# A two-layer transformer kernel whose order comes from a planner: own PSUM bank for the transposes of x, three early loads of x, a split last F pair, quartered output, and a new table of priorities

## The chip, the cores and the metric

The kernel runs on one core of a Trainium2 chip. The metric is device time in microseconds for one execution, lower is better; the profile's span, from the first to the last instruction, is a little shorter. PE is the matrix engine (PEld its weight loads), DVE the vector engine, ACT the scalar engine, POOL GpSimd, and SP the engine that here issues all DMAs.

## What is computed

Two kinds of layer alternate, four in all, on x of 2048 rows and 512 columns, float32:

```python
x = x + attention(layernorm(x), wqkv) @ wo          # 32 heads of 16; each row sees 8 rows: itself, -2, -4, ... -14
x = x + (gelu(xn @ w_gate) * (xn @ w_up)) @ w_down  # xn = layernorm(x), F = 1792
# the same two again, with the same weights
```

The text calls one attention and one feed-forward together a layer: layer 0 and layer 1.

## The kernel before

**Chunks.** Attention steps by 2, so even and odd rows never mix. `CHUNKS` (L38) cuts each layer into 8 chunks of 256 rows of one parity, each of J = 2 tiles of 128 rows. A chunk goes through three stages, for each of which a function adds nodes to a graph: `attention_inputs` (L1015), `attention` (L1092), `feed_forward` (L1229).

**Precision by halves.** Every product is made of float16 parts: an operand is split into hi and lo, and hi*hi + hi*lo + lo*hi is summed (`passes`, L1008), three matmuls for one. Weights are scaled by a power of two from their largest value, then split into hi and lo: `absmax` and `abssum` (L561, L570) find the largest value or a bound, `exponents` (L460) turns it across the partitions with PE, `split` (L513) makes hi on ACT (L520) and lo on DVE (L525). Activations are split and transposed in `split_transpose` (L955): ACT copies hi (L962), POOL subtracts lo (L966), then a DMA transposes both (L971), or, for the first tiles (`pt` = 6 of them), PE does (L981) and ACT copies the result from PSUM to `ax` (L988).

**attention_inputs.** x is loaded (`load_xa`, L824; into the buffers `x` instead of `xa` for the chunks in `early`, L1429), normed (statistics on DVE, L880; a chain of small steps on POOL, L937 to L952; ACT applies it, L1000), split, transposed, and multiplied by w_qkv in halves h of the heads: per tile and h two banks of `pg`, 512 and 256 columns (L1050). ACT copies them to `sc` (L1076), and SP stores them to DRAM as `qkvd` (L1085).

**attention.** For each of 4 groups of 8 heads SP loads q, k and v with the windows' rows (L1115), DVE multiplies and sums (L1138, L1147), softmax follows on DVE and ACT, DVE multiplies by v and sums (L1205, L1217). All products go through `prod`, one buffer of 128 x 2048 float32. The result is split and transposed into `ot`, one buffer.

**feed_forward.** PE multiplies `ot` by w_o (L1011, 512 columns), DVE adds to x (L1254), a second norm and transpose give `bx`. Then 7 pairs u of F blocks: gate and up on PE (L1011, 24 matmuls of 256 columns each), gelu on ACT (L1305), the product on DVE (L1312), sums of blocks on POOL (L1322 to L1324), which make 7 blocks out of 4 for a scheme with 7 products in place of 8, hi on ACT (L1332) and lo on POOL (L1337) into one of three buffers `gh`, and 21 matmuls with w_down into the banks `pd` (L1346). After the last pair DVE gathers six times from `pd` into x (L1375), and SP stores it (L1388): to `xs` after layer 0, to the output after layer 1, for the last chunk in two pieces.

w_down's raw rows are likewise turned into 7 blocks (`prep_d`, L694): for five pairs in place, and for the last two in halves s of 128 columns, with a temporary buffer each (L756: s = 0 in the second `bx`, s = 1 in `sc`).

**PSUM.** Eight banks: three `pg` of its own, one `pe` for the softmax, four `pd`. Until 196 us of the plan (`retire`), the four `pd` serve as other things: pd0, pd1 and pd3 as three more buffers of `pg`, pd2 as `pt`, which takes the transposes of x (L981), those of `exponents` (L473) and the warming matmuls (`unread`, L1407, L1411). Names in the profile are those of the bank, so a projection into one of them reads `pd`.

**What sets the order.** `Graph.plan` (L206) is a list scheduler that runs when the kernel is built: of all nodes whose inputs are there it takes the one that can start first by its cost model, and among those that can start together the one of lowest priority number. Costs are `t_act`, `t_dve`, `t_dvp`, `t_pool`, `t_mm` (L296 to L317), and `LAG` (L104) is the time from an instruction's end until another engine may use its result. The table `AT` (L52) holds the priorities: for instance `x0` for x of chunk 0, `lq0` and `lq1` for the loads of w_qkv, `pq`, `pf`, `po`, `pd` for the preparation of the weights, `start` and `step` for the chunks' own time T. Each engine then runs its list in order; semaphores come from the data.

## Time and profile before

| | |
|---|---|
| median of 3 runs | 1246.38 us (1244.66 to 1246.49) |
| profiled execution, its own time | 1246.04 us |
| its span | 1244.3 us |
| granted clock of PE, mean | 0.987 |
| idle time of PE in the span | 43.5 us |
| moved by DMA | 174.76 MB, 140 GB/s over the span |

A row of instructions gives line, engine, operation, output <- input, shape and count, then busy time, mean of one in ns, idle time of the engine before them and what ended it. A row of waits gives who waited for whom: time in total, times, longest. A row of a timeline gives start, length and instructions merged. SPq is SP's issuing of DMAs, "DMA bx<-hl" a transfer.

### The profile page before, as it was taken

The numbers are of one execution on the slowest core, as the hardware profiler recorded it, in microseconds if no ns is written. First come the engines' busy times: TensorE is split into PE (matmuls) and PEld (weight loads), VectorE is DVE, ScalarE is ACT, GpSimd is POOL, SyncE is SP. The second block draws the span as 40 slices with busy tenths as digits, with TensorE's granted clock in tenths as the row PEclk, the third lists the DMA queues.
The fourth block names the chain that finished last, engine by engine and source line by source line (L and its number), as shares of the span: only waits on it lengthen the run. The fifth ranks groups of instructions, "written<-read, shape, count | busy, mean of one in ns | idle before, by whom it ended". The sixth has DMA issues, their size and how long they took to land.

```text
span 1244.3 us, 24043 instructions
## 1 busy us (share of the span) xinstructions
PE 1200.8 (97%) x9722; PEld 954.1 (77%) x9722; DVE 935.5 (75%) x972; ACT 542.0 (44%) x911; POOL 690.2 (55%) x839
## 2 busy tenths in 40 slices
PE   3899989999999999999999999999999999999997
PEld 1455658887888778885688878878788888788886
DVE  7999998799868988517877867789788688775121
ACT  5787654434443435323443433434352625343211
POOL 3233426665666458553485936765476657465543
PEclk7899999999999999999999999999999999999999
DMA  9878783345533494208923346343834344241000
GB/s 337 280 246 202 205 224 117 128 146 144 159 115 127 137 252 107 94 2 232 235 96 100 128 138 165 101 145 115 241 104 118 100 132 124 100 124 43 18 18 18
DMA packets 195791, 174.76 MB, mean 140 GB/s; under 512 B 101904, under 2 KB 162656, under 8 KB 195680
## 3 DMA queue, kind: packets, MB, share of 16 engines
q1 hardware_dynamic: 195680, 173.23, 47.8%
q8 instruction: 76, 1.25, 0.4%
q14 instruction: 35, 0.29, 0.1%
HBM read 115.87 MB, written 33.73 MB: 120 GB/s over the span
## 4 chain that ended last, share of the span: by engine, by line
PE 84%; DMA 5%; DVE 4%; POOL 3%; issue 2%; ACT 1%; SPq 0%; POOLq 0%; DVEq 0%; ACTq 0%
PE pg L1011 51%; PE pd L1346 20%; PE pg L1050 9%; PE pd L1050 3%; DMA ax<-hl 2%; POOL hl L966 1%; DMA bx<-hl 1%; DMA xa<-xs 1%; DMA ot<-hl 1%; PE pd L1011 1%; DMA kv<-qkvd 1%; DVE prod L1138 1%; DMA w_d<-in_A_wqkv_dram 1%; POOL nw L938 0%; DVE w_q L525 0%
## 5 line engine op out<-in xcount | busy, mean ns | idle before, releaser
L1011 PE MATMUL pg<-bx,w_g 128*128 128x256 f16 x2664 | 310.6, 273 | 5.1 <-DMA bx<-hl 5.1
L1011 PE MATMUL pg<-bx,w_u 128*128 128x256 f16 x2664 | 309.0, 273 | 0.0
L1011 PEld LDWEIGHTS <-w_g 128*128 128x128 f16 x2688 | 263.6, 98 | 39.2 <-issue 5.6
L1011 PEld LDWEIGHTS <-w_u 128*128 128x128 f16 x2688 | 263.0, 98 | 30.6
L1050 PEld LDWEIGHTS <-ax 128*128 128x128 f16 x1536 | 151.5, 99 | 111.0 <-issue 12.0
L1050 PE MATMUL pg<-w_q,ax 128*128 128x512 f16 (+1 forms) x1152 | 203.0, 334 | 6.3 <-DVE w_q L525 4.2
L1312 DVE SCALAR_TENSOR_TENSOR sc<-pg,small,sc 128x512 f32<-128x512 f32 (+1 forms) x127 | 85.1, 680 | 157.7 <-PE pg L1011 143.1
L1305 ACT ACTIVATE sc<-pg,small 128x512 f32<-128x512 f32 (+1 forms) x127 | 78.8, 633 | 224.3 <-PE pg L1011 186.7
L1217 DVE TENSOR_REDUCE o<-prod 128x256 f32<-128x2048 f32 x64 | 146.1, 2282 | 36.2 <-POOL hl L966 33.7
L1322 POOL TENSOR_TENSOR sc<-sc 128x256 f32<-128x256 f32 x112 | 100.4, 896 | 127.0 <-DVE sc L1312 120.9
L1138 DVE TENSOR_TENSOR prod<-kv,q 128x2048 f32<-128x2048 f32 x64 | 152.6, 2385 | 7.8 <-DMA kv<-qkvd 7.1
L1205 DVE TENSOR_TENSOR prod<-kv,pe 128x1024 f32<-128x1024 f32 x128 | 152.6, 1216 | 1.4
L1147 DVE TENSOR_REDUCE lg<-prod 128x128 f32<-128x2048 f32 x64 | 145.7, 2277 | 0.6
L966 POOL TENSOR_TENSOR hl<-o,hl 128x256 f16<-128x256 f32 x64 | 59.2, 926 | 109.9 <-ACT hl L962 109.5
L1337 POOL TENSOR_TENSOR w_u<-sc,w_u 128x896 f16<-128x896 f32 x37 | 78.0, 2108 | 32.9 <-ACT w_u L1332 32.8
L1375 DVE SCALAR_TENSOR_TENSOR x<-pd,small,x 128x512 f32<-128x512 f32 x96 | 70.5, 743 | 32.9 <-PE pd L1346 31.4
L1337 POOL TENSOR_TENSOR w_g<-sc,w_g 128x896 f16<-128x896 f32 x37 | 76.2, 2059 | 32.7 <-ACT w_g L1332 32.4
L1346 PE MATMUL pd<-w_d,gh 128*128 128x256 f16 x798 | 93.5, 273 | 0.0
L1337 POOL TENSOR_TENSOR gh<-sc,gh 128x896 f16<-128x896 f32 x38 | 76.1, 2003 | 29.8 <-ACT gh L1332 29.6
L1346 PE MATMUL pd<-w_d,w_u 128*128 128x256 f16 x777 | 91.0, 273 | 0.0
L1346 PE MATMUL pd<-w_d,w_g 128*128 128x256 f16 x777 | 90.9, 273 | 0.0
L1324 POOL TENSOR_TENSOR sc<-sc 128x256 f32<-128x256 f32 x112 | 83.6, 747 | 8.8
(126 smaller groups left out, 1395.2 us busy)
## 6 DMA issues: line engine op xcount, KB each, us to landing
kv<-qkvd SPq DMA_DIRECT2D x128, 576.0 KB, 3.9
qkvd<-sc SPq DMA_DIRECT2D x64, 384.0 KB, 3.9
q<-qkvd SPq DMA_DIRECT2D x64, 128.0 KB, 3.5
x<-in_A_x_dram SPq DMA_DIRECT2D x9, 512.0 KB, 5.5
xs<-x SPq DMA_DIRECT2D x8, 512.0 KB, 4.8
xa<-xs SPq DMA_DIRECT2D x16, 256.0 KB, 3.8
x<-xs SPq DMA_DIRECT2D x8, 512.0 KB, 4.6
xa<-in_A_x_dram SPq DMA_DIRECT2D x14, 256.0 KB, 4.5
```

Source lines behind the costliest of these rows:

```text
L1011: nc.tensor.matmul(pt, a, b, start=i == 0, stop=i == n - 1)
L1050: nc.tensor.matmul(pgs[n].tile()[:, 0 : hi - lo], a[:, i // 2, kt], part(h * KT + kt)[:, lo:hi], start=(i, kt) == (0, 0), stop=(i, kt) == ...
L1138: nc.vector.tensor_mul(prod, win, q.tile().unsqueeze(2).to_broadcast([P, J, W, P]))
L1147: lambda lgv=lgv, heads=heads: nc.vector.tensor_reduce(lgv()[:, :, heads].rearrange("p j h w -> p j w h"), prod.rearrange("p j w (h d) -> ...
L1205: nc.vector.tensor_mul(paired[:, j].rearrange("p q (h d) t -> p q t h d", d=DH), win, by.unsqueeze(4).to_broadcast([P, W // 2, 2, HPG, DH]),)
L1217: lambda o=o: nc.vector.tensor_reduce(o.tile(), paired.rearrange("p j q c t -> p j c q t"), axis=AX.XY, op=ALU.add),
L1305: lambda sel=sel, h=h, part=part, g_of=g_of: nc.scalar.activation(g_of()[:, sel], part(0, sel), AF.Gelu_apprx_tanh, scale=cst["s_gate", h],),
L1312: lambda sel=sel, h=h, part=part, g_of=g_of: nc.vector.scalar_tensor_tensor(g_of()[:, sel], part(1, sel), cst["c_up", h], g_of()[:, sel], ...
L1322: tt(b[:, 4:6], b[:, 0:2], b[:, 3:4].to_broadcast([P, 2, P]), op=ALU.add)
L1324: tt(b[:, 1:3], b[:, 1:3], b[:, 0:4:3], op=ALU.subtract)
L1337: lambda blocks=blocks, gh_of=gh_of: nc.gpsimd.tensor_sub(gh_of()[:, 1], blocks(), gh_of()[:, 0]),
L1346: nc.tensor.matmul(pds_[PD_AT[m][0]].tile()[:, PD_AT[m][1]], gh_of()[:, a, G_AT[m]], wd_of(u, m, b), start=u == 0 and n == 0 and PD_AT[m][ ...
```

## The change

The pieces, in the order of the diff:

- `AT` has new values throughout and new entries: an offset for each chunk's inputs, attention and feed-forward (`I`, `A`, `F` with layer and chunk), for its groups of heads (`B`), for each pair of w_down (`D`), and a second value (`_2`) of 16 knobs, which holds from chunk 4 of layer 0 on (`turn` = 4; `knob` reads it).
- The planner's costs: DVE's and ACT's instructions are shorter by about 0.08 and 0.1 us, and their results come later by as much.
- `pg` has five buffers in the first stretch instead of six; pd3 becomes `px`, which takes the transposes of x alone. `retire` is at 161.55 us.
- The second halves of the last two pairs of w_down take `prod` as their temporary buffer.
- The first nodes of PE-transposed splits, the transposes, the gate and up matmuls, and the gelus are each kept in program order; w_o's product is planned after x has been asked for.
- `early` = 2: x of chunks 1 and 2 is loaded into the buffers `x`, that of chunk 0 as before into `xa`.
- In the last pair of the last chunk, blocks 0 and 3, which the sums leave as they are, get hi and lo ahead of the sums; the products 4 and 3, which need these alone, no longer wait for the other blocks.
- The output of the last chunk is stored in four quarters (a tile's 256 columns each) as each is gathered, the last of them by ACT.

Some priorities as they come out of the table, before and after: x of chunk 0 -1647 and -2454 (its two tiles), after -6653 and -6508; first load of w_qkv -6025, after -5513; w_o -1505, after -3790; gate matmuls of chunk 0 from 137, after from 2653; first projections of chunk 5 (-18.49 + 138.98 x 10 + 981.86 - 329.66 + 164.47) at 2188, their second half 740 later; those of chunk 6 (856.27 + 183.11 x 12 - 1471.81 + 1267.42 + 164.47) at 3014.

The core of the diff:

```diff
-    lq0=-6024.71, lq1=-3848.17, lf0=-1122.81, lo=-1504.86, lf1=-880.86, ld=-724.89, pq0=-2261.26, pq1=1109.7,
-    pf0=-58.05, po=-50.3, pf1=863.38, pd=596.57, x0=-1647.47, first=117.89, tile=80.47, ahead=10.4, lead=1240.39,
...
+    lq0=-5512.9, lq1=-2937.45, lf0=-1635.77, lo=-3790.27, lf1=-2793.33, ld=5813.67, pq0=-2542.65, pq1=-5324.02,
+    pf0=-2904.78, po=2529.52, pf1=-399.99, pd=3361.46, x0=-8823.93, first=-18.49, tile=138.98, ahead=10.4,
+    lead=3679.49, norm=10434.96, proj=164.47, half=740.13, row=247.98, att=-1559.49, hg1=-5.5, hg2=-93.36,
...
-LAG = {"PE": 0.25, "DVE": 0.07, "ACT": 0.1, "POOL": 0.12, "SP": 0.0}
+LAG = {"PE": 0.25, "DVE": 0.15, "ACT": 0.2, "POOL": 0.16, "SP": 0.0}
...
-    return 0.19 + 0.093 * ptr + n / 1200
+    return 0.09 + 0.093 * ptr + n / 1200
...
-    return (n + 151) / 960
+    return (n + 72) / 960
...
     P_pg = Pool(
-        "pg", [ps.tile([P, 512], F32, name=f"pg{i}") for i in range(3)] + banks(pds[0], pds[1], pds[3]),
+        "pg", [ps.tile([P, 512], F32, name=f"pg{i}") for i in range(3)] + banks(pds[0], pds[1]),
         fifo=False,
     )
     P_pt = Pool("pt", banks(pds[2]), fifo=False)
+    P_px = Pool("px", banks(pds[3]), fifo=False)
...
-            at = prio + AT["pdu"] * u
+            at = prio + AT["pdu"] * u + AT.get(f"D{u}", 0)
...
             for s in range(2):
-                sc = Lease(P_sc) if s else Lease(P_bx, only=(1,))
+                sc = Lease(P_pr) if s else Lease(P_bx, only=(1,))
                 blocks = lambda sc=sc, s=s: (
-                    sc.tile() if s else sc.tile().rearrange("p j t k c -> p (j t k c)").bitcast(F32)[:, 0 : 7 * P]
-                ).rearrange("p (m c) -> p m c", m=7)
+                    sc.tile().rearrange("p j w c -> p (j w c)") if s
+                    else sc.tile().rearrange("p j t k c -> p (j t k c)").bitcast(F32)
+                )[:, 0 : 7 * P].rearrange("p (m c) -> p m c", m=7)
                 cols_of = slice(s * P, (s + 1) * P)
...
+    def knob(name, l, c):
+        return AT.get(name + "_2", AT[name]) if 8 * l + c >= AT.get("turn", 4) else AT[name]
...
+    heads, turned_last, in_turn = [], [], {}
...
-        g.add(
+        first = g.add(
             "ACT", t_act(n), lambda: nc.scalar.copy(hi(), src()),
-            r=src_keys, w=[(lease, 0)], get=[lease], prio=prio,
-        )
+            r=src_keys, w=[(lease, 0)], get=[lease], prio=prio, order=heads[-1:] if on == "PE" else (),
+        )
+        if on == "PE":
+            heads.append(first)
         g.add(
...
-        pt = Lease(P_pt)
+        pt = Lease(P_px)
...
             "PE", 2 * nb * 0.06, turn, r=[(lease, 0), (lease, 1)], w=[(pt, 0)], get=[pt], prio=prio, urgent=True,
+            order=turned_last[-1:],
         ))
+        turned_last.append(turns[-1])
...
-                g.add(
+                in_turn["pg"] = g.add(
                     "PE", 24 * t_mm(N), columns,
                     r=[*((bx, j) for j in range(J)), *((key, h * KT + k) for h in hs for k in range(KT))],
-                    w=[(pgs[n], 0)], get=[pgs[n]], prio=T + AT["gu"] * J * u + 0.01 * n,
+                    w=[(pgs[n], 0)], get=[pgs[n]], prio=T + knob("gu", l, c) * J * u + 0.01 * n,
+                    order=[in_turn.get("pg")],
...
+            direct = last and u == NU - 1
+            if direct:
+                ends = lambda t: t[:, 0:4:3]
+                g.add(
+                    "ACT", t_act(2 * P),
+                    lambda blocks=blocks, gh_of=gh_of: nc.scalar.copy(ends(gh_of()[:, 0]), ends(blocks())),
+                    r=gk, w=[(gh, 0, 0)], get=[gh], prio=ev,
+                )
+                g.add(
+                    "POOL", t_pool(2 * P),
+                    lambda blocks=blocks, gh_of=gh_of: nc.gpsimd.tensor_sub(
+                        ends(gh_of()[:, 1]), ends(blocks()), ends(gh_of()[:, 0])
+                    ),
+                    r=[*gk, (gh, 0, 0)], w=[(gh, 1, 0)], prio=ev,
+                )
             if u >= AT["sd"]:
                 g.add("POOL", 2 * t_pool(2 * P) + t_pool(P) + 0.21, sums, w=gk, prio=ev)
             else:
                 g.add("DVE port", 2 * t_dve(2 * P) + t_dve(P), sums, w=gk, prio=ev)
-            g.add(
-                "ACT", t_act(7 * P),
-                lambda blocks=blocks, gh_of=gh_of: nc.scalar.copy(gh_of()[:, 0], blocks()),
-                r=gk, w=[(gh, 0)], get=[] if hold else [gh], prio=ev,
-            )
-            g.add(
-                "POOL", t_pool(7 * P),
-                lambda blocks=blocks, gh_of=gh_of: nc.gpsimd.tensor_sub(
-                    gh_of()[:, 1], blocks(), gh_of()[:, 0]
-                ),
-                r=[*gk, (gh, 0)], w=[(gh, 1)], prio=ev,
-            )
+            for k, cut in enumerate((slice(1, 3), slice(4, 7)) if direct else (slice(0, 7),)):
+                n = (cut.stop - cut.start) * P
+                g.add(
+                    "ACT", t_act(n),
+                    lambda blocks=blocks, gh_of=gh_of, cut=cut: nc.scalar.copy(gh_of()[:, 0, cut], blocks()[:, cut]),
+                    r=gk, w=[(gh, 0, k + direct)], get=[] if hold or direct else [gh], prio=ev,
+                )
+                g.add(
+                    "POOL", t_pool(n),
+                    lambda blocks=blocks, gh_of=gh_of, cut=cut: nc.gpsimd.tensor_sub(
+                        gh_of()[:, 1, cut], blocks()[:, cut], gh_of()[:, 0, cut]
+                    ),
+                    r=[*gk, (gh, 0, k + direct)], w=[(gh, 1, k + direct)], prio=ev,
+                )
 
...
             order = [4, 3, 5, 2, 7, 6, 1]
-            lag = AT["late_end"] if last else AT["late"]
+            lag = AT["late_end"] if last else knob("late", l, c)
             for ms in [order[k : k + 2] for k in range(0, 7, 2)] if u in (0, NU - 1) else [order]:
                 i = PD_AT[ms[0]][0]
+                need = [k for k in range(3) if not direct and k == 0 or direct and (k == 0) == (i == 0)]
                 g.add(
                     "PE", 3 * len(ms) * t_mm(HD), lambda ms=ms, down=down: down(ms),
-                    r=[(gh, 0), (gh, 1), *(("d", u, s, a) for s in range(2) for a in range(2)), ("su_d", 0)],
+                    r=[*((gh, a, k) for a in range(2) for k in need), *(("d", u, s, a) for s in range(2) for a in range(2)), ("su_d", 0)],
                     w=[(pds_[PD_AT[m][0]], m) for m in ms], get=[pds_[i]] if u == 0 else [],
                     order=retire[i : i + 1] if u == 0 else [],
-                    prio=T + AT["gu"] * J * (u + 1) + lag - 0.5,
+                    prio=T + knob("gu", l, c) * J * (u + 1) + lag - 0.5,
                 )
...
-                "DVE", t_dvp(D), gather, r=[(pds_[PD_AT[m][0]], m) for m in {*of}], w=[(xl, j) for j in range(J)], prio=T - 2500,
-            )
-
-        for js in [slice(j, j + 1) for j in range(J)] if last else [slice(0, J)]:
-            n = js.stop - js.start
-            g.add(
-                "SP", T_ISSUE + 0.1,
-                lambda js=js: nc.sync.dma_start(
-                    rows(xs if l == 0 else out, l, c)[:, js], xl.tile()[:, js]
-                ),
-                r=[(xl, j) for j in range(js.start, js.stop)],
-                w=pieces(0, c) if l == 0 else [("out", c, js.start)],
-                kb=268 * n, prio=T - 3000, urgent=True, fixed=1.1,
+                "DVE", t_dvp(D), gather, r=[(pds_[PD_AT[m][0]], m) for m in {*of}],
+                w=[*((xl, j) for j in range(J)), *((xl, "b", k) for k in to)], prio=T - 2500,
+            )
+
+        to_of = lambda: rows(xs if l == 0 else out, l, c)
+        if last:
+            for k in (1, 2, 0, 3):
+                j, half = k // 2, slice(k % 2 * HD, (k % 2 + 1) * HD)
+                g.add(
+                    "ACT" if k == 3 else "SP", T_ISSUE + 0.1,
+                    lambda j=j, half=half, on=nc.scalar if k == 3 else nc.sync: on.dma_start(
+                        to_of()[:, j, half], xl.tile()[:, j, half]
+                    ),
+                    r=[(xl, "b", k)], w=[("out", c, k)], kb=134, prio=T - 3000, urgent=True, fixed=1.1,
+                )
+        else:
+            g.add(
+                "SP", T_ISSUE + 0.1, lambda: nc.sync.dma_start(to_of(), xl.tile()[:, 0:J]),
+                r=[(xl, "b", k) for k in range(2 * J)], w=pieces(0, c) if l == 0 else [("out", c)],
+                kb=268 * J, prio=T - 3000, urgent=True, fixed=1.1,
             )
...
-    for q, i in ((P_pg, 3), (P_pg, 4), (P_pt, 0), (P_pg, 5)):
+    for q, i in ((P_pg, 3), (P_pg, 4), (P_pt, 0), (P_px, 0)):
...
-                when = t - AT["lead"]
-            attention_inputs(l, c, when)
-            ot, mark = attention(l, c, t)
-            feed_forward(l, c, t, ot, mark)
-            t += AT["step"] * J
+                when = t - knob("lead", l, c)
+            attention_inputs(l, c, when + AT.get(f"I{l}{c}", 0))
+            ot, mark = attention(l, c, t + AT.get(f"A{l}{c}", 0))
+            feed_forward(l, c, t + AT.get(f"F{l}{c}", 0), ot, mark)
+            t += knob("step", l, c) * J
+            if 8 * l + c + 1 == AT.get("turn", 4) and "start_2" in AT:
+                t = AT["start_2"] + knob("step", 1, 0) * (tiles + J)
             tiles += J
 
...
-    retire[2].order.extend(turns)
+    for n in retire[2:]:
+        n.order.extend(t for t in turns if t is not n)
```

58 lines of the change are left out of this document (35 added, 23 removed).

## The prediction

> **What bounds the kernel now.** I read the page's first lines, then a table of busy time by stretch, then the matmuls of the first stretch alone, and last the chain and the timelines at the two ends. The page first:
>
> ```profile
> span 1244.3 us, 24043 instructions
> PE 1200.8 (97%) x9722; PEld 954.1 (77%) x9722; DVE 935.5 (75%) x972; ACT 542.0 (44%) x911; POOL 690.2 (55%) x839
> ```
>
> PE is the bound, but 97% says little: an instruction counts as busy while it drains beneath the next. The table by stretch (length, then busy time of PE, PEld, DVE, ACT, POOL, granted clock, DMA share, GB/s) shows where PE isn't covered:
>
> ```profile
> 0.00:29.95 29.95, 10.35 (x23) 3.75 (x23) 21.06 (x43) 16.33 (x29) 9.62 (x38) 0.77 0.94 334
> 29.95:60.00 30.05, 24.45 (x135) 14.39 (x134) 27.88 (x47) 25.17 (x41) 6.69 (x6) 0.84 0.84 281
> 60.00:100.00 40.00, 37.17 (x229) 22.00 (x228) 35.56 (x53) 29.68 (x60) 12.99 (x26) 0.95 0.83 257
> 100.00:186.10 86.10, 79.95 (x485) 47.10 (x483) 80.64 (x99) 55.60 (x102) 28.55 (x49) 1.00 0.81 204
> 186.10:240.00 53.90, 53.89 (x455) 45.37 (x456) 43.06 (x41) 23.92 (x38) 35.84 (x40) 0.97 0.38 122
> 240.00:560.00 320.00, 319.82 (x2744) 268.23 (x2742) 244.45 (x239) 128.30 (x205) 197.90 (x242) 1.00 0.44 129
> 560.00:620.00 60.00, 57.74 (x373) 36.08 (x371) 48.17 (x42) 27.24 (x56) 21.86 (x29) 1.00 0.91 240
> 620.00:1140.00 520.00, 520.00 (x4424) 432.43 (x4422) 415.31 (x385) 209.49 (x345) 325.68 (x355) 1.00 0.43 123
> 1140.00:1237.40 97.40, 97.40 (x870) 84.77 (x867) 16.55 (x25) 26.24 (x41) 51.02 (x59) 1.00 0.06 17
> 1237.40:1244.30 6.90, 0.03 (x1) 0.00 (x0) 2.85 (x4) 0.00 (x0) 0.00 (x0) 0.80 0.20 76
> ```
>
> From 186 to 1237 us PE is idle for only 2.5 us, at the turn from layer 0 to layer 1. What can be won lies in the first 186 us and the last 7. Now the work itself, by pace. Two rows of the chain give it, 12 matmuls of 512 columns and 192 of 256 (start, length):
>
> ```profile
> 160.74 2.59 PE pd L1011 x12
> ...
> 372.40 20.96 PE pg L1011 x192
> ```
>
> That is 0.1092 us for 256 columns, 0.2158 for 512. By the code there are 16 x 7 x 48 gate and up, 16 x 7 x 21 down and 768 projection matmuls of 256, 8496 in all, and 768 + 384 of 512. So 927.8 + 248.6 = 1176.4 us is streaming, which the change leaves as it is. How much of it is done by 186.1 us, when the first gate matmul starts, the groups of that stretch say:
>
> ```profile
> L1050 PE MATMUL pg<-w_q,ax 128*128 128x512 f16 x240 | 61.2, 395 | 4.9 <-DVE w_q L525 4.2 <-DMA ax<-hl 0.6
> L1050 PE MATMUL pd<-w_q,ax 128*128 128x512 f16 x144 | 34.2, 390 | 1.6 <-DMA ax<-hl 1.6
> L1050 PE MATMUL pd<-w_q,ax 128*128 128x256 f16 x240 | 31.0, 276 | 0.0
> L1050 PE MATMUL pg<-w_q,ax 128*128 128x256 f16 x144 | 19.8, 275 | 0.0
> ...
> L1011 PE MATMUL pd<-w_o,ot 128*128 128x512 f16 x12 | 2.8, 379 | 0.0
> L1011 PE MATMUL pg<-w_o,ot 128*128 128x512 f16 x12 | 2.8, 379 | 0.0
> ```
>
> 384 + 24 of 512 columns and 384 of 256: 88.1 + 41.9 = 130.0 us. These are all 16 tiles of layer 0: PE has used up its filler when the first feed-forward begins, and even waits for it. The span is thus 130.0 work + **56.1 lost before 186.1** + 1046.4 work + 4.9 lost up to 1237.4 + 6.9 of tail = 1244.3 us. The profiled execution took 1246.04 us, 1.74 beyond its span; the median of the three runs, 1246.38, is 0.34 above it.
>
> **The change, part by part. The start.** Before:
>
> ```profile
> 0.72 5.80 SPq L558 DMA_DIRECT2D w_d<-in_A_wqkv_dram  x8
> ...
> 7.75 1.48 SPq L834 DMA_DIRECT2D xa<-in_A_x_dram  x2
> ```
>
> ```profile
> 4.08 0.95 DVE L564 TENSOR_REDUCE small<-w_d 128x1 f32<-128x768 f32 x1 [4.08 <-DMA w_d<-in_A_wqkv_dram]
> ...
> 13.23 3.80 DVE L525 SCALAR_TENSOR_TENSOR w_q<-w_d,small,w_q 128x768 f16<-128x768 f32 x4
> 16.95 1.28 DVE L880 BATCH_NORM_STATS2 nw<-xa 128x6 f32<-128x512 f32 x2
> ```
>
> ```profile
> 27.89 0.99 ACT L988 COPY ax<-pd 128x1024 f16<-128x1024 f16 x1
> ```
>
> ```profile
> 29.95 0.63 PE L1050 MATMUL pg<-w_q,ax 128*128 128x512 f16 x1
> ```
>
> SP issues eight loads of w_qkv, then x of chunk 0; DVE takes its statistics at 16.95, after the fourth lo half of the weights; 11.9 us later the transposed x is copied (27.89 + 0.99), and the first projection starts at 29.95. In the changed table of priorities x of chunk 0 stands at -8823.93 + 2170.66 = -6653, ahead of lq0 = -5512.9; before it was -1647 behind -6025. Planned so, SP issues x first: two issues of 0.74 us, so w_qkv comes 1.5 us later (its fourth lo half at 17.0 + 1.5 = 18.5). The first load of all reached DVE 3.4 us after its issue; x needs about as long, say 5 us with the second piece, and 11.9 us of norm, split, transpose and copy end at 17 to 18. The first projection can start at 18.5 instead of 29.95: **-11.4 us**. The price of the 1.5 us on w_qkv is in that; the 512 KB moved forward don't grow.
>
> It pays only if the feed-forward moves too, as no filler is left. So DVE decides, which prepares weights and does attention. Up to its last reduction for chunk 1 at 212.1 us:
>
> ```profile
> 9.50:212.10 202.60, 172.66 (x1084) 108.41 (x1084) 185.97 (x261) 134.75 (x239) 72.40 (x123) 0.92 0.79 236
> ```
>
> ```profile
> 234.00 2.59 SPq L971 DMA_TRANSPOSE bx<-hl  x2
> ```
>
> ```profile
> 243.38 2.78 PE L1011 MATMUL pg<-bx,w_g 128*128 128x256 f16 x24
> ```
>
> DVE idles 16.6 us of 202.6. Chunk 1's input to the feed-forward is transposed until 236.6 and its landing is close ahead of its first gate matmul at 243.38, so both chunks must come earlier, by at most about 16.6 us if DVE is never idle. 11.4 fits, and not much more. Of the 56.1 us I take 11.4 off and leave the rest.
>
> **Transposes in a bank of their own.** What it removes:
>
> ```profile
> PE pd L1411 <- ACT ax L988: 2.7, 1, 2.7
> ```
>
> ```profile
> PE pg L1050 <- DVE w_q L525: 4.2, 2, 2.6
> ...
> PE pd L981 <- ACT ax L988: 1.1, 1, 1.1
> ```
>
> The warming matmuls of L1411 waited for the ax copy because they shared its bank: 2.7 us, inside the 29.95 already counted, and 1.1 us later. I book nothing extra: behind that 1.1 the 4.2 us wait for the lo halves ends last. It costs pg one of six banks in the first stretch. A half tile fills two banks in 12 x (0.216 + 0.109) = 3.9 us of PE, and no PE wait on ACT's evacuation stands among the groups above, so 5 should do; bounds 0 to the 3.9 us of one half tile; I take 0. If ACT's copies are late in the new order, the cover is gone.
>
> **x of three chunks.** Its second load takes the other buffer of x, which chunk 0's feed-forward wants much later (wo starts at 160.74). That is 512 KB sooner, in a stretch with the DMA at 0.94, against weights that DVE wants: from 0 to 1.6 us, its transfer time at the 334 GB/s of the first stretch; I take 0, since it only swaps the order of loads that DVE reaches later.
>
> **Order and costs.** New costs make an operation shorter and its result later by the same 0.08 to 0.1 us (LAG): priorities only. The order within layer 1's start gets knobs of its own: of the 2.5 us idle there I take **-1**.
>
> **The tail.** The last pair's gh waits for its buffer, not for data, and PE then runs through:
>
> ```profile
> 1230.52 0.94 ACT L1332 CAST gh<-sc 128x896 f16<-128x896 f32 x1 [1.35 <-PE pd L1346]
> ```
>
> ```profile
> 1235.83 4.63 DVE L1375 SCALAR_TENSOR_TENSOR x<-pd,small,x 128x512 f32<-128x512 f32 x6 [9.02 <-PE pd L1346]
> ```
>
> ```profile
> 1240.49 0.83 SPq L1388 DMA_DIRECT2D out_dram<-x  x2
> ```
>
> ```profile
> out_dram<-x SPq DMA_DIRECT2D x2, 256.0 KB, 2.4
> ```
>
> Splitting the unsummed blocks first costs one more fixed part on ACT and POOL, and lets PE do products 4 and 3 earlier; the first two of DVE's six gathers (0.77 us each) can then run beside PE. But PE's total is the same, and four gathers still follow. After PE's end at 1237.4 DVE goes on to 1240.46, of which one gather must follow: 0.77 to 3.1 us, so 0 to -2.3; I take -0.75. The last two quarters go out on two queues at once: it saves SP's second issue, 0.83 / 2 = 0.4 us, and some of the landing: 0 to -1.2; I take -0.75. An issue by ACT isn't in the trace; the first SP issue of the run (0.72 to 4.08) against the 2.4 us above bounds its extra at 1 us. Tail: **-1.5**. On this the Trainium skill, "DMA: Bandwidth & Descriptors", section "Issuing engines are not separate DMA queues", says that issuing from several engines saves only the sequencer's time. By that rule alone the second half would be -0.4, and the total 0.35 us higher; no run so far has output on two queues.
>
> **Sum:** 1244.3 - 11.4 - 1 - 1.5 = 1230.4; + 1.74 = 1232.1; + 0.34 gives **1232 us**.
>
> **The rivals.** *More than that.* The clock: PE waits 4.58 us ahead of 186.11, and its first 24 matmuls then take 4.45 us instead of 2.62:
>
> ```profile
> 186.11 4.45 PE L1011 MATMUL pg<-bx,w_g 128*128 128x256 f16 x24 [4.58 <-DMA bx<-hl]
> ```
>
> If the order closes this wait (4.6 + 1.8), the 4.2 us for w_q, and leaves some tiles of layer 0 for later as filler, 1232 - 10.6 = 1221, down to 1212 when all of DVE's idle time goes. For: layer 0's projections were all spent early, and the new priorities set chunk 6 (3014) and the second halves of chunk 5 (2928) behind the first gate matmuls (2653). Against: DVE is 92% busy already.
>
> *Nothing moves.* x comes early, but PE only waits longer at 186; then the tail and the turn alone count: 1246.4 - 2.5 = 1244, 1241 to 1248. For: PE stood waiting for bx.
>
> *Slower.* The second halves of the last two pairs of w_down are now prepared in prod, the one buffer through which all attention products pass; before they lay in a buffer of sc:
>
> ```profile
> 135.73 0.28 DVE L706 TENSOR_TENSOR sc<-sc 128x128 f32<-128x128 f32 x1
> ...
> 155.66 1.55 DVE L731 TENSOR_TENSOR w_d<-sc,w_d 128x896 f16<-128x896 f32 x1
> ```
>
> One such buffer was held for 21 us. While prod is held so, attention stands still on DVE. Two holds of 10 us, with chunk 1 waiting, cost 20 and give 1232 + 20 = 1252; 1249 to 1262. It decides from about 14 us of holding that nothing else on DVE fills. For: the hold falls into the same 200 us as the attention of chunks 0 and 1. Against: sums, cast and subtraction alone are some 4 us, and DVE has other work there.
>
> **Chances.** Forecast (1224 to 1241) 0.50; more 0.21; nothing moves 0.09, a third of it below 1244; slower 0.20. The range 1214 to 1250 leaves out the far part of "more" and most of "slower". A measurement tells about 0.2%, 2.5 us, from no change: faster 0.74, same 0.06, slower 0.20.
>
> **What would show it.** Start: the first L1050 matmul at 18 to 20 us, x issued ahead of w_qkv. Feed-forward: first gate matmul near 175, chunk 1's near 232, DVE idling under 8 us between 9.5 and its last reduction of chunk 1. Bank: no wait of L1411 or L981 on L988, none of L1050 on L1076 over 1 us. Tail: 5.4 us instead of 6.9 after the last matmul. Wrong it is if the first projection starts after 25 us, if PE is idle for over 3 us anywhere between 200 and 1230, or if L1138 or L1205 wait while prod holds w_down.

## The result, and the profile after

The changed kernel is slower: a median of 1255.14 us (1247.77 to 1256.86 in ten runs) against 1245.65 of the kernel before on the same chip (1244.65 to 1250.88), a ratio of 1.0061 (95% interval 1.0040 to 1.0081). The prediction was 1232 us. The profiled execution took 1256.17 us; its page begins (span, then busy time and share of each engine):

```profile
span 1254.1 us, 24038 instructions
PE 1203.7 (96%) x9722; PEld 954.2 (76%) x9722; DVE 951.7 (76%) x972; ACT 548.7 (44%) x919; POOL 694.8 (55%) x841
```

The same matmuls, 9.8 us more span; DVE's 972 instructions take 16.2 us longer. Where it went is shown by the table of stretches, cut at this kernel's own events (columns as in the prediction: length, then busy time of PE, PEld, DVE, ACT, POOL, granted clock, DMA share, GB/s):

```profile
163.81:220.00 56.19, 55.59 (x475) 46.25 (x473) 49.28 (x60) 31.66 (x47) 32.85 (x29) 1.00 0.12 40
220.00:260.00 40.00, 32.89 (x261) 26.73 (x260) 31.72 (x36) 17.84 (x27) 18.27 (x22) 0.91 0.30 90
...
300.00:500.00 200.00, 193.02 (x1541) 151.23 (x1540) 174.24 (x159) 88.24 (x150) 108.90 (x139) 0.99 0.61 165
...
780.00:860.00 80.00, 76.23 (x608) 59.77 (x607) 51.17 (x44) 30.21 (x49) 41.62 (x44) 0.98 0.52 143
```

Look at PE against the length. The first gate matmul now starts at 163.81 us instead of 186.11. But where the kernel before covered everything from 186 us on, PE now has holes at 220 to 260, 300 to 500 and 780 to 860. Busy time flatters PE, so from here on a stretch's loss is its length less its streaming work, by the prediction's 0.1092 us for 256 columns and 0.2158 for 512, each matmul counted in the stretch in which it starts. All 9648 of these matmuls are in both traces, so the sums are span less 1176.4 us; the edges leave some 0.2 us a stretch open. (The expectations below use a rougher count, in which matmuls at the edges stand twice: 10.2 for the 10.4 at 220 to 260, 16 for the 18.6 behind 260, 2.3 for the 2.8 of the kernel before at 560 to 620 and 6.2 for its 6.4 at 160 to 220.)

| lost, us | 0–220 | 220–260 | 260–560 | 560–1200 | tail from 1200 | sum |
|---|---|---|---|---|---|---|
| before | 57.7 | 0.0 | 0.3 | 2.9 | 7.0 | 67.9 |
| after | 42.3 | 10.4 | 10.3 | 8.3 | 6.3 | 77.7 |

Up to 220 us 15.4 us less are lost, more than forecast. From there to 1200 us 25.8 us are lost that the kernel before doesn't lose. PE's waits between 160 and 1240 us say by whom (waiting line, then what ended the wait; total, times, longest; the largest of them):

```profile
PE pg L1033 <- DMA bx<-hl: 9.0, 4, 5.1
PE pg L1033 <- ACT pe L1201: 2.6, 1, 2.6
PE pg L1033 <- DVE sc L1336: 2.0, 1, 2.0
PE pd L1387 <- POOL w_g L1378: 1.6, 1, 1.6
PE pd L1387 <- DVE w_d L743: 1.5, 2, 0.9
PE pd L1387 <- ACT w_d L740: 1.1, 1, 1.1
```

DMA, ACT, DVE and POOL all stand here, mostly once each: no one engine is late, each is late somewhere. The longest wait stands ahead of the second chunk's first gate matmul. PE's timeline there (start, length, instructions merged, idle time before):

```profile
209.93 2.78 PE L1033 MATMUL pg<-bx,w_u 128*128 128x256 f16 x24
...
230.42 2.34 PE L1387 MATMUL pd<-w_d,gh 128*128 128x256 f16 x20 [0.86 <-DVE w_d L743]
237.87 5.30 PE L1033 MATMUL pg<-bx,w_g 128*128 128x256 f16 x24 [5.10 <-DMA bx<-hl]
```

The first chunk's last up matmuls end at 212.7; its last w_down products, two projections in between, fill PE until 232.8; then it waits 5.10 us, and the next 24 matmuls take 5.30 us instead of 2.78. What stood between shows on POOL and ACT:

```profile
217.69 2.45 POOL L1348 TENSOR_TENSOR sc<-sc 128x256 f32<-128x256 f32 x1
221.19 1.89 POOL L1378 TENSOR_TENSOR gh<-sc,gh 128x896 f16<-128x896 f32 x1 [1.05 <-ACT gh L1373]
223.17 0.91 POOL L951 TENSOR_SCALAR nw<-nw 128x2 f32<-128x2 f32 x1
...
227.15 0.20 POOL L965 TENSOR_TENSOR nw<-nw 128x2 f32<-128x2 f32 x1
231.24 3.58 POOL L986 TENSOR_TENSOR hl<-sc,hl 128x512 f16<-128x512 f32 x2 [3.90 <-ACT hl L980]
```

```profile
227.21 0.93 ACT L740 CAST w_d<-bx 128x896 f16<-128x896 f32 x1
...
228.31 0.94 ACT L740 CAST w_d<-prod 128x896 f16<-128x896 f32 x1
229.14 1.52 ACT L1022 ACTIVATE sc<-x,nw 128x512 f32<-128x512 f32 x2
```

The second chunk's norm (L951 to L965) runs on POOL behind the sums and the split of the first chunk's last pair, and its application (L1022) on ACT behind w_down's last copies. In the kernel before, w_o's product for that chunk came with two pairs still to go instead of one, and its norm stood on POOL ahead of the sums of the last pair but one:

```profile
230.48 0.20 POOL L949 TENSOR_TENSOR nw<-nw 128x2 f32<-128x2 f32 x1
230.78 0.84 POOL L1322 TENSOR_TENSOR sc<-sc 128x256 f32<-128x256 f32 x1
```

So the first chunk's feed-forward moved by 22.3 us and the second's by 5.5 (243.38 to 237.87). It was not DVE's attention that held the second chunk. Its last reduction, the split of that result on POOL and w_o's product after, and the reduction and w_o's product before:

```profile
173.47 2.27 DVE L1239 TENSOR_REDUCE o<-prod 128x256 f32<-128x2048 f32 x1
192.69 0.67 POOL L986 TENSOR_TENSOR hl<-o,hl 128x256 f16<-128x256 f32 x1
197.54 5.34 PE L1033 MATMUL pg<-w_o,ot 128*128 128x512 f16 x24
```

```profile
209.79 2.28 DVE L1217 TENSOR_REDUCE o<-prod 128x256 f32<-128x2048 f32 x1
218.55 5.34 PE L1011 MATMUL pg<-w_o,ot 128*128 128x512 f16 x24
```

DVE is done 36.3 us sooner, w_o's product starts 21.0 us sooner, the gate matmuls 5.5. The split stands on POOL behind the sums of other pairs, 17 us after its input is there; from w_o's product to the gate matmuls it then takes 40.3 us instead of 24.8. Part of this stands in the order itself: the plan that the kernel makes when it is built leaves PE idle for 5.4 us between 220 and 260 us, and for nothing from 260 to 1200.

### The profile page after: what moved, and what is told of

Its sections match the earlier page's. It is cut to its first block, busy times and chain, and to the rows that moved or that the text cites. A ratio compares the mean times of both kernels' runs of the same rounds, so it can differ in the third digit from the quotient of the medians.

```text
span 1254.1 us, 24038 instructions
## 1 busy us (share of the span) xinstructions
PE 1203.7 (96%) x9722; PEld 954.2 (76%) x9722; DVE 951.7 (76%) x972; ACT 548.7 (44%) x919; POOL 694.8 (55%) x841
## 4 chain that ended last, share of the span: by engine, by line
PE 57%; DVE 17%; POOL 9%; DMA 8%; issue 5%; ACT 3%; SPq 1%; POOLq 0%; ACTq 0%; DVEq 0%
PE pg L1033 37%; PE pd L1387 15%; PE pg L1072 4%; DVE prod L1160 3%; DMA ax<-hl 3%; DVE o L1239 2%; DVE prod L1227 2%; POOL sc L1346 2%; DVE lg L1169 2%; POOL hl L986 2%; DMA xa<-xs 1%; DMA xs<-x 1%; DVE small L576 1%; DMA bx<-hl 1%; DVE x L1417 1%
## 5 line engine op out<-in xcount | busy, mean ns | idle before, releaser
L1033 PE MATMUL pg<-bx,w_g 128*128 128x256 f16 x2688 | 315.9, 275 | 13.6 <-DMA bx<-hl 9.0
L1033 PE MATMUL pg<-bx,w_u 128*128 128x256 f16 x2688 | 312.6, 273 | 0.7 <-ACT sc L1328 0.7
L1072 PE MATMUL pg<-w_q,ax 128*128 128x256 f16 (+1 forms) x1260 | 218.2, 330 | 10.8 <-DMA ax<-hl 4.5
L1346 POOL TENSOR_TENSOR sc<-sc 128x256 f32<-128x256 f32 x112 | 99.1, 885 | 142.3 <-DVE sc L1336 132.8
L1160 DVE TENSOR_TENSOR prod<-kv,q 128x2048 f32<-128x2048 f32 x64 | 161.4, 2521 | 18.1 <-DMA kv<-qkvd 13.7
L986 POOL TENSOR_TENSOR hl<-o,hl 128x256 f16<-128x256 f32 x64 | 51.4, 803 | 123.6 <-ACT hl L980 123.5
L1378 POOL TENSOR_TENSOR gh<-sc,gh 128x896 f16<-128x896 f32 (+2 forms) x39 | 82.2, 2108 | 31.0 <-ACT gh L1373 30.9
L1348 POOL TENSOR_TENSOR sc<-sc 128x256 f32<-128x256 f32 x112 | 93.3, 833 | 8.8
L1378 POOL TENSOR_TENSOR w_u<-sc,w_u 128x896 f16<-128x896 f32 x37 | 73.7, 1992 | 33.1 <-ACT w_u L1373 33.0
L1378 POOL TENSOR_TENSOR w_g<-sc,w_g 128x896 f16<-128x896 f32 x37 | 72.7, 1964 | 34.0 <-ACT w_g L1373 34.0
L1387 PEld LDWEIGHTS <-gh 128*128 128x128 f16 x798 | 77.9, 98 | 13.9 <-issue 2.4
```

The lines of the kernel that those rows point to most:

```text
L1033: nc.tensor.matmul(pt, a, b, start=i == 0, stop=i == n - 1)
L1072: nc.tensor.matmul(pgs[n].tile()[:, 0 : hi - lo], a[:, i // 2, kt], part(h * KT + kt)[:, lo:hi], start=(i, kt) == (0, 0), stop=(i, kt) == ...
L1160: nc.vector.tensor_mul(prod, win, q.tile().unsqueeze(2).to_broadcast([P, J, W, P]))
L1346: tt(b[:, 4:6], b[:, 0:2], b[:, 3:4].to_broadcast([P, 2, P]), op=ALU.add)
L1348: tt(b[:, 1:3], b[:, 1:3], b[:, 0:4:3], op=ALU.subtract)
L1378: lambda blocks=blocks, gh_of=gh_of, cut=cut: nc.gpsimd.tensor_sub(gh_of()[:, 1, cut], blocks()[:, cut], gh_of()[:, 0, cut]),
```

## The experiments

The theories after the first look: 1, DVE has lost its lead over PE, since PE starts 22 us earlier and DVE does not; 2, POOL's chain is late, and slows DVE where both run; 3, the DMA's landings are late. (The rows above already speak against the last words of 1, up to the second chunk: there DVE's attention did come earlier.) The later expectations each name their own theory 1. Unless said otherwise the order of every engine's list is frozen, and only instructions change. "Before" is the kernel before, run beside each; the ratios are to it. A stretch table comes from one execution of each kernel.

**The tail by itself** (the kernel before with the split last pair and the quartered output, nothing else).

> The kernel before with only the change's end: the last pair's blocks 0 and 3 split ahead of the sums, and the last chunk stored in quarters, the last by ACT. The order up to 1220 us is that of before. By the prediction's tail step it gains 1.5 us, from 6.9 us after the last matmul to 5.4. By the trace of the changed kernel (6.1 us there, its six gathers still in one run after the last products) it gains 0.8. If the second queue costs time, it is slower by up to 1.

Measured: 1245.1 us (1242.86 to 1247.55), ratio 0.9989 (0.9978 to 0.9999); the tail loses 6.3 us instead of 7.0. The loss is not in this part of the change.

**Three reliefs on the changed kernel.**

```diff
-  win = [..., [P, J], [P, W], [1, P]];       prod <- win * q        # DVE: 8 window rows
+  win = [..., [P, J], [P, W // 2], [1, P]];  prod[:, :, :W//2] <- .. # 4
...
+  k = P if l + c == 0 else 32                 # POOL: block sums on 32 of 128 columns
-  dma_start(kv, n * P)                        # DMA: k and v
+  dma_start(kv, n * P // 4)                   # a quarter, after the first chunk
```

> The changed kernel in the same order on every engine, but q times k is formed for 4 of the 8 rows of a window only (the sums take what lies in prod): 64 DVE instructions of half the length, some 70 us less for DVE. Theory 1: since the feed-forward starts 22 us earlier, DVE has no lead left in layer 0 and every delay on it reaches PE; then the stalls from 220 to 500 us (about 17 us) go and the time falls to about 1238. Theory 2 (POOL's chain of sums, split and norm, and its port shared with DVE, is late) and theory 3 (DMA transposes that land in 5 to 7 us instead of 2.7 are late): 2 to 5 us at most, the stalls near 314, 470 and 810 us stay.

> The changed kernel in the same order, but from the second chunk on POOL forms the sums of blocks on 32 of 128 columns only: of some 247 us of POOL's time about 160 go. Theory 2 (POOL is late, and its port holds DVE up): the stalls after 260 us go, 1255 falls to about 1243, and DVE's q times k returns from 2.52 us to 2.3. Theory 1 (DVE): a gain only as far as DVE is held up less, 2 to 4 us. Theory 3 (DMA): under 2 us.

> The changed kernel in the same order, but k and v are loaded at a quarter of their length after the first chunk: some 50 MB of 175 less on the DMA engines. Theory 3 (transposes and loads land late because the DMA engines are loaded): bx, ax and ot land in under 3 us throughout, the stalls after 300 us go and 1255 falls to about 1243; the wait at 237 us stays. Theories 1 and 2: under 3 us of gain.

Measured: DVE 1236.28 us, ratio 0.9923 (0.9911 to 0.9936); POOL 1243.04, 0.9974 (0.9964 to 0.9983); DMA 1239.77, 0.9947 (0.9934 to 0.9960). By stretch:

| lost, us | 0–220 | 220–260 | 260–560 | 560–1200 |
|---|---|---|---|---|
| after | 42.3 | 10.4 | 10.3 | 8.3 |
| half of q·k | 37.7 | 8.1 | 2.1 | 3.9 |
| quarter of POOL's sums | 42.8 | 11.2 | 2.7 | 3.6 |
| quarter of k, v | 40.4 | 9.7 | 1.7 | 2.1 |

Each of three unlike reliefs takes away most of the 18.6 us lost behind 260 (3.8 to 6.3 stay, and the kernel before loses 3.2 there), and none the loss at 220 to 260. The stretch from 300 to 500 us, in the same three kernels in that order, is nearly full again:

```profile
300.00:500.00 200.00, 198.00 (x1629) 159.12 (x1628) 162.41 (x163) 90.74 (x152) 112.08 (x148) 1.00 0.62 167
```

```profile
300.00:500.00 200.00, 197.59 (x1597) 156.03 (x1596) 177.46 (x164) 93.62 (x157) 96.77 (x146) 1.00 0.62 168
```

```profile
300.00:500.00 200.00, 198.54 (x1619) 158.17 (x1618) 175.69 (x165) 93.09 (x156) 123.53 (x148) 1.00 0.43 106
```

All three theories, each naming one late engine, fall as stated, since each gave the other two reliefs little. Two of their signs failed as well: q·k on DVE fell from 2.52 us to 2.48 with POOL's relief, not to 2.3, and with the shorter loads a transpose of `bx` still took up to 6.5 us to land. The reading that is left is a chain through all of them without slack. That reliefs work through one another's engine is not excluded, but the 2.48 and, with the shorter loads, 2.43 us of q·k show little of it.

**The same reliefs on the kernel before**, as a control.

> The kernel before, order the same; the q.k product runs over 4 of the 8 window rows, so VectorE has some 75 us less work. Theory 1 (the kernel before has its engines ahead of TensorE from 186 us on, so that relief is worth nothing there): what it gains is gained ahead of 186 us, at most 4 products of 1.2 us, so 1240 to 1246, and the stages from 220 us on lose what they lost, 7 to 10 us with the tail. Theory 2 (VectorE holds both kernels alike): it gains what the changed kernel gained by it, 19 us, so 1225 to 1230.

> The kernel before, order the same, loads of k and v at a quarter of their length after the first chunk. Theory 1: nothing that a run can tell, 1242 to 1247, since its loads land ahead of need. Theory 2 (late landings cost both kernels alike): 15 us less, as in the changed kernel, so 1229 to 1233.

Measured: with half of q·k 1244.72 us, ratio 0.9983 (0.9972 to 0.9994), as theory 1 had it: in its trace the four stretches up to 1200 us lose 58.8, 0.0, 0.3 and 2.4, so behind 220 us nothing to speak of is gained, where the same relief took 14.9 us off the changed kernel. This is the control: the same load of DVE costs time in the new order and not in the old. With shorter k and v 1238.87, 0.9937 (0.9918 to 0.9955), a miss for both: the gain is no 15 us, but not nothing. Before 220 us it loses 53.7 instead of 57.7, and at the turn (560 to 620) 2.4 less; in between PE was full before and is full now (200.00 us busy of the 200 from 300 on). Two pairs can then be compared. With half of q·k in both, the change is worth -8.4 us (1236.28 against 1244.72, on two chips; -7.5 by the ratios): in the two traces 21.1 us less are lost ahead of 220, 8.1 more at 220 to 260, 3.3 more from 260 to 1200. With shorter loads it is worth +0.9 us (+1.2 by the ratios): the 13.3 us that it wins ahead of 220 are lost at 220 to 260 (9.7) and in small pieces behind it (3.7).

**w_down's sums shortened.** The second chunk's norm waits on ACT and POOL for instructions that wait in turn for DVE's sums of w_down (L718 to L721), which in this kernel run inside the first feed-forward:

```diff
-  tt(b[:, 0], b[:, 3], b[:, 6], op=ALU.add)  ...
+  b = b[:, :, 0:32] if b.shape[2] == HD else b   # first five pairs
+  tt(b[:, 0], b[:, 3], b[:, 6], op=ALU.add)  ...
```

> The changed kernel, every engine's order the same; the sums that VectorE makes for the first five pairs of w_down (lines 718 to 721) run over 32 of the 256 columns, the other columns stay unsummed. Theory 1 (the new order puts w_down's preparation into the first chunk's feed-forward, and the second chunk's norm and split stand behind it on ScalarE and GpSimd, which wait for those sums): the 10.2 us lost between 220 and 260 us fall below 3, the 15 us lost between 300 and 860 stay within 4 of it, and the run takes 1244 to 1249. Theory 2 (the second chunk's feed-forward waits for its own attention or for the transposes' landing, not for w_down): 8 to 11 us are still lost at 220 to 260 and the run stays within 0.2% of the changed kernel.

> The changed kernel, order the same, with both reliefs: the sums of w_down's first five pairs over 32 of 256 columns, and the loads of k and v at a quarter of their length after the first chunk. If the two losses are separate and additive (theory 1), it takes 1226 to 1233, about the 1229 that the start alone would give, with less than 6 us lost between 220 and 1200. If the relief only moves the wait to a later stage (theory 2), it stays at 1235 to 1240, as with the shorter loads alone.

Measured: 1249.26 us (1248.3 to 1253.58), ratio 1.0025 (1.0013 to 1.0036), and with the shorter loads 1237.19, 0.9921 (0.9897 to 0.9944): no sum of the two. The first kernel gained 5.9 us, more than its theory 2 allows; the two together came out as theory 2 had it. The rows come from one more run of each:

> The same kernel as in the run with w_down's sums over 32 of 256 columns, once more for its trace by stage. That run took 1249.26 us, 5.9 less than the changed kernel. Theory 1 (w_down's preparation in front of the second chunk's norm and split): the wait ahead of that chunk's first gate matmul falls from 5.1 us to under 1, and the 10.2 us lost between 220 and 260 us to under 4. Rival (the gain came from later stages, and the second chunk waits for something else): 8 to 11 us stay lost at 220 to 260.

> The same kernel as in the run with both reliefs (w_down's sums over 32 of 256 columns; k and v loads at a quarter of their length after the first chunk), once more for its trace by stage. It took 1237.19 us against 1239.77 with the shorter loads alone, so the reliefs did not add up. If the second chunk's wait merely moves on to the next stage, 220 to 260 us shows under 4 us lost and a stage behind it 4 to 8 more than with the shorter loads alone; if something else than the sums holds the second chunk, 220 to 260 still shows 6 to 9.

These took 1253.36 and 1238.02 us. A sum now takes 0.60 us or less, and the wait has not moved; DVE's row, then PE's:

```profile
199.47 0.60 DVE L719 TENSOR_TENSOR w_d<-w_d 128x32 f32<-128x32 f32 x1
```

```profile
238.29 4.02 PE L1034 MATMUL pg<-bx,w_g 128*128 128x256 f16 x18 [5.09 <-DMA bx<-hl]
```

At 220 to 260 us 8.2 and 7.8 us stay lost; in the first run of the same two kernels it was 7.8 and 7.4, with the same wait of 5.1 us. (Of the first kernel these two executions also show how far one kernel's stretches differ: 41.1 and 44.8 us up to 220, under 1 us behind it.) My theory that the sums hold the second chunk is refuted: they cost 2 to 3 of the 10.4 us. In this trace the last pair's product on DVE waits for PE's up matmuls, and the norm follows that pair's split on POOL, as in the changed kernel: the chunk is held by its place behind PE's own last pair. That is read from the trace, not tested. Moving the norm alone was not run, since the second chunk's transposes also wait for the `bx` buffer that w_down's last halves leave only at 229 us; which of the two would be next isn't settled.

**The wait filled with work.** 36 extra matmuls, 3.9 us, ahead of the second chunk's first gate matmul:

```diff
+  fill = (l, c, u, n) == (0, 1, 0, 0)
+  for i in range(3 if fill else 0):
+      passes(pg.tile()[:, 0:N], 12 products of w_g and the first chunk's bx)
```

> The changed kernel, order the same; right ahead of the second chunk's first gate matmul, into the same bank, PE gets 36 extra matmuls of 256 columns on data of the first chunk, whose sums are overwritten: 3.9 us of work inside the 5.1 us wait. Theory 1 (the wait costs its own length and then the half pace behind it): the 24 gate matmuls after it take 2.6 to 2.9 us in place of 5.3, the loss between 220 and 260 counts 2 to 3 us less (the extra matmuls counted as lost), and the run takes 1251 to 1254. Rival (what is late behind the wait is late anyway, since VectorE and not PE sets the pace there): the gate matmuls are quicker, the time stays within 0.1% of the changed kernel, and the gain comes back as waits between 240 and 340 us.

Measured: 1249.6 us (1244.21 to 1250.78), ratio 1.0013 (0.9999 to 1.0028), 5.5 less than the changed kernel. On PE:

```profile
234.66 4.09 PE L1033 MATMUL pg<-bx,w_g 128*128 128x256 f16 x36
239.90 2.79 PE L1033 MATMUL pg<-bx,w_g 128*128 128x256 f16 x24 [1.15 <-DMA bx<-hl]
```

The gate matmuls behind the wait run at full pace, 2.79 us in place of 5.30; the loss at 220 to 260 is 4.3 + 3.9 of filling = 8.2, 2.2 less than 10.4, as theory 1 had it. The rest of the 5.5 is later (260 to 560 loses 6.5 instead of 10.3, 560 to 1200 7.2 instead of 8.3), and more than I expected.

**prod set free.** The prediction's slower rival had the size (1249 to 1262), and the trace does show prod held by w_down's halves: ACT's first scaling into it is at 177.75, DVE's next attention product at 230.41.

```profile
229.28 1.09 DVE L743 TENSOR_TENSOR w_d<-prod,w_d 128x896 f16<-128x896 f32 x1
230.41 2.29 DVE L1160 TENSOR_TENSOR prod<-kv,q 128x2048 f32<-128x2048 f32 x1
```

```profile
186.36:230.41 44.05, 41.46 (x330) 32.14 (x329) 34.56 (x41) 24.83 (x37) 28.97 (x27) 1.00 0.07 21
```

In 44 us DVE is idle for 9.5, of which it waits 6.7 for ACT's copies of w_d and 2.5 for POOL. The two halves follow each other in prod, the second from 225.07 on. So seven nodes were moved in the lists:

```diff
+  staging and sums of the half in prod: from 178.8, 180.8, 183.7 to 212.5, 212.6, 213.65
+  first q.k product and reduction of the third chunk: from 231.85, 234.73 to 183.75, 183.8
+  next loads of k and q: from 234.2, 234.7 to 190.0, 190.1
```

> The changed kernel with seven places of its order changed: the staging of w_down's half in prod (two scalings on ScalarE, the sums on VectorE, planned from 179 to 184 us) goes behind 212 us, just ahead of its use; the first q.k product and reduction of the third chunk, planned at 232 to 235 us though q and k have landed by 170, take its place at 184 us, and the next loads of k and q follow at 190. In the changed kernel prod is held by w_down from 178 to 230 us, and VectorE waits 9.5 us between 186 and 230. If that hold costs the time (the prediction's rival), VectorE does 4.5 us of attention in those waits, the loss behind 260 us falls by 4 to 8 and the run takes 1247 to 1251. If VectorE's work on w_down is itself what the second chunk and the last pairs of the first wait for (theory 1), the attention moved ahead delays it: the loss at 220 to 260 rises from 10 to 11 to 15, behind 260 it falls by less than 2, and the run takes 1254 to 1260.

Measured: 1257.27 us (1250.69 to 1258.47), ratio 1.0096 (1.0079 to 1.0113). DVE did the product early, at 184.60 us. The median did not fall, so the hold up to 212 us is not what costs the time. The edit left a hold: w_down's two halves still fill prod from 214.5 to 234.6 us, and that part was not freed. In the profiled execution, the fastest of this kernel, 220 to 260 still loses 10.3 us (theory 1 said 11 to 15, too much), and 300 to 400 loses 0.9 instead of 5.4, which the medians don't confirm.

**Orders with margin.** Tables of priorities chosen not by the planned end but by replaying the lists with the mean durations of the two traces and random delays. Two keep the start of the kernel before (with the new tail), one the early start with the filled wait; the fourth fills the first wait of all in the first of them.

```diff
+  AT.update(... 55 or 143 priorities ...)
+  MARGIN["PE"], MARGIN["SP"], DMA_FIXED = 0.91, 1.15, 2.42    # second table; 0.7, 0.0, 1.4 before
```

These three are what the planner allows: ahead of PE's and SP's work, and for a landing. In the first table they are 0.72, 0.06 and 0.27, in the early start's 0.73, 0.0 and 2.22, so planned ends of different tables don't rest on the same costs.

> Structure and start of the kernel before with the split last pair and the quartered output; a new table of priorities, chosen not by the planned end but by replaying the order with the two traces' mean durations plus random delays of engines and landings, so that it holds margin. It is planned to end at 1239.6 us, later than the changed kernel's 1229.8. Theory 1 (margin against late results decides, not the planned end): it slips by under 5 us behind its plan and takes 1239 to 1244, with under 1 us lost at 560 to 620 (the kernel before loses 2.3) and at 220 to 1200 in all. Rival (the planned end decides, the changed kernel only had bad luck in one place): it takes 1246 to 1250, as the order with the later planned end.

> Another table chosen in the same way, planned to end at 1238.2 us; in the replay it also closes most of the wait ahead of the first gate matmul. Theory 1: 1237 to 1242, with 1 to 3 us lost between 160 and 220 us where the kernel before loses 6.2, and under 2 us between 220 and 1200. Rival: as the kernel before, 1244 to 1248, the gain at 160 to 220 given back behind it.

> The kernel with the margin table (the first of this call), order the same, with 36 extra matmuls of 256 columns ahead of the first gate matmul of all, into the same bank, overwritten after. If idle time in front of that matmul costs half pace behind it, as the 4.45 us of 24 matmuls in the kernel before and 5.30 us in the changed kernel showed, this takes 1 to 2 us less than the same kernel without them; if the first feed-forward is not limited by PE there, 0.

> Structure and early start of the changed kernel, its table altered by the same search (planned end 1236.1 us, 6.3 later than the changed kernel's plan), and the 36 extra matmuls ahead of the second chunk's first gate matmul. Theory 1 (the early start is worth having once the order behind it holds margin): the loss up to 220 us stays 10 us or more under the kernel before, 220 to 260 still loses 6 to 10, behind that under 7 in place of the changed kernel's 16, so 1240 to 1247. Rival (what the early start wins is lost again whatever the order, since the engines that feed PE have no more to give): 10 us or more lost behind 260 us, and 1248 to 1255.

| kernel | us (range) | ratio to before (95%) | lost 0–220 | 220–260 | 260–560 | 560–1200 |
|---|---|---|---|---|---|---|
| tail by itself (above) | 1245.1 (1242.86–1247.55) | 0.9989 (0.9978–0.9999) | 59.2 | 0.0 | -0.1 | 3.2 |
| first table | 1244.42 (1242.84–1245.44) | 0.9991 (0.9982–1.0001) | 55.1 | 0.2 | 4.6 | -0.1 |
| second table | 1242.01 (1238.55–1244.31) | 0.9968 (0.9956–0.9980) | 55.3 | -0.1 | 1.1 | 0.6 |
| first table, filled | 1246.04 (1244.58–1249.56) | 1.0008 (0.9997–1.0019) | 50.1 + 3.9 | 0.0 | 6.1 | -0.1 |
| early start, filled | 1250.54 (1246.72–1253.93) | 1.0041 (1.0025–1.0057) | 42.9 | 5.2 + 3.9 | 6.5 | 3.5 |

The second table, planned to end at 1238.2 us where the changed kernel's plan ends at 1229.8, is the fastest that computes everything, 3.6 us under the kernel before and 13 under the changed one. About 1 us of the 3.6 is the tail, which these tables have too. The first table gains nothing beyond it, a miss for both sides: 1244.42 lies outside 1239 to 1244 as well as 1246 to 1250, and 4.7 us are lost from 220 to 1200 instead of under 1. The second reaches the upper end of its 1237 to 1242, with 4.7 us lost at 160 to 220 instead of 1 to 3. So one table of two speaks for margin, and with the kernel before's late start; theory 1 is not shown. The early start with another order stays slow, no faster than the changed kernel with the same filling (1249.6), which is the rival's side: its profiled run, again its fastest, loses 19.1 us behind 220 with the filling. That start was not worth having under any order tried. Filling the first wait was a miss. It gives the pace back at once:

```profile
183.94 4.12 PE L1023 MATMUL pg<-bx,w_g 128*128 128x256 f16 x24 [3.97 <-DMA bx<-hl]
```

```profile
184.07 2.79 PE L1023 MATMUL pg<-bx,w_g 128*128 128x256 f16 x24 [0.56 <-DMA bx<-hl]
```

But PE, 1.3 us ahead, waits longer for the next transposes of `ot`, which release it at 343.6 us in both traces: 4.0 us instead of 1.2.

## Why the prediction was wrong

**The start was right in kind, and a second gain came on top.** Booked: -11.4 us, first projection at 18.5. SP now issues x at once, w_qkv behind it, and PE's first projection follows at 14.89:

```profile
0.73 0.87 SPq L850 DMA_DIRECT2D xa<-in_A_x_dram  x2
1.64 6.24 SPq L570 DMA_DIRECT2D w_d<-in_A_wqkv_dram  x8
```

```profile
14.89 0.48 PE L1072 MATMUL pg<-w_q,ax 128*128 128x512 f16 x2 [0.70 <-ACT w_q L532]
```

Up to 160 us 10.0 us less are lost (41.3 instead of 51.3), about what was booked. The other 5.4 of the 15.4 come between 160 and 220, where the wait of 4.58 us ahead of the first gate matmul is gone:

```profile
163.81 2.78 PE L1033 MATMUL pg<-bx,w_g 128*128 128x256 f16 x24
```

The prediction had this wait under its rival "more" and did not book it.

**"DVE decides ... 11.4 fits, and not much more" was wrong in its reason.** The prediction asked that both chunks come earlier. The first gate matmul came at 163.81 (forecast near 175), the second chunk's at 237.87 (forecast near 232). The bound of 16.6 us took all that DVE did up to 212.1 us as needed for chunk 1. The new order puts w_down's preparation behind chunk 1's attention, at 176 to 230 us, and DVE ends that attention 36.3 us sooner, with 10.7 us idle from 9.5 us on (the forecast asked for under 8):

```profile
9.50:175.74 166.24, 149.06 (x925) 90.27 (x924) 155.57 (x214) 106.50 (x204) 62.92 (x104) 0.98 0.94 286
```

So DVE had the time, and the lists behind it gave the lead back before the second gate. DVE pays later: its first reduction of the third chunk starts at 259.19 us instead of 241.14.

**The step that failed** is the one behind it: "Of the 56.1 us I take 11.4 off and leave the rest", together with the sum, which carries "1046.4 work + 4.9 lost up to 1237.4" over from the kernel before less 1 us for the turn. Those small losses were a property of the old order, in which PE was late enough for everything else to be ahead. Moved forward, PE meets the others: the forecast's -1 between 220 and 1200 us was +25.8 (10.4 of it at 220 to 260). Behind 260 us the reliefs and their controls show it; for 220 to 260 the cause is read from the trace and stays untested. The stretch 240 to 560 shows it on DVE, 282 us busy where the kernel before had 244 (in the table of the prediction):

```profile
240.00:560.00 320.00, 312.49 (x2587) 254.63 (x2586) 282.43 (x255) 135.26 (x220) 193.82 (x228) 0.99 0.54 149
```

DVE's load alone isn't the cause: with the shorter loads it is busy for 285 us of the same stretch, and only 1.7 us are lost from 260 to 560.

I had the rule in the text, "Wrong it is if ... PE is idle for over 3 us anywhere between 200 and 1230", as a test and gave it no term in the sum. The prediction should have asked, chunk by chunk, how long before PE's need each input lands, and booked what an earlier need leaves uncovered.

**The smaller steps.** The turn: PE is idle for 1.2 us at 560 to 620 instead of 2.3, as booked (-1). The tail: 6.1 us after the last matmul instead of 6.9, -0.8 of -1.5; the six gathers still run as one row that starts 1.6 us ahead of PE's end, as before, and the two queues are there:

```profile
1245.51 2.46 PE L1387 MATMUL pd<-w_d,gh 128*128 128x256 f16 x21
1246.36 4.63 DVE L1417 SCALAR_TENSOR_TENSOR x<-pd,small,x 128x512 f32<-128x512 f32 x6 [6.62 <-PE pd L1387]
1248.66 2.70 SPq L1433 DMA_DIRECT2D out_dram<-x  x3
1251.03 0.38 ACTq L1433 DMA_DIRECT2D out_dram<-x  x1
```

The -0.75 for gathers beside PE did not come. The bank: projections wait at most 0.8 us for ACT's evacuation, so five buffers of `pg` do, as booked; but the transposes still wait for the copy out of their one bank, 3.3 us at 61.90, which the prediction had excluded.

```profile
61.90 0.61 PE L1001 MATMUL pd<-ident,hl 128*128 128x128 f16 x8 [3.32 <-ACT ax L1010]
```

**The rivals.** "Slower" had the time (1249 to 1262), but by luck: prod was held once for 47 us and once for 5, not twice for 10, and attention done inside the long hold gained nothing. "More" was right that the wait ahead of the first gate matmul closes, and assumed that what is won there is kept. "Nothing moves" had PE wait longer at 186 us; it started at 163.81.

## What to carry to other kernels

A bound engine with no idle time behind a point tells that the others are ahead of it there, not how far: before an earlier start is booked, take for each later chunk the gap between the landing of its input and its use, and subtract. An engine that finishes its part sooner isn't enough: follow the input through every list up to the bound engine, since each can give the lead back (36.3 us on DVE became 5.5 on PE). If several unlike reliefs all help, and one of them does nothing in the kernel before, look at the slack of the order rather than for one late engine. A planned end didn't tell which order runs faster: here the plan was 9.0 us shorter (1229.8 against 1238.8) and the run 9.5 us longer. Whether margin in the planner helps is open. Filling a wait with work can win PE's pace back, but that pays only if the next input is early.
